# Reordering loads, casts and transposes in the first two batches of an attention + MoE kernel

## The chip, the cores and the metric

The kernel runs on one core of a Trainium2 chip. The metric is the device time of one execution in microseconds (us). Each kernel was executed four times or more, the kernel before beside it on the same chip; medians are quoted, and the spread of one kernel is mostly about 1%.

Names used below: PE is the TensorE, PEld its weight loads, DVE the VectorE, ACT the ScalarE, POOL the GpSimd, SP the engine that issues most DMAs. "The software queue" is the DMA queue that POOL issues to (q0 in the profile), "the hardware queue" the one that SP issues to (q1). Both feed the same 16 DMA engines: from 20 to 40 us of the kernel before, the profile gives them shares of 89.8% and 33.9% of these 16 (a share adds up the time that packets took, so two can exceed 100% together).

## The reference

```python
# q, k, v: (8 batches, 8 heads, 576 tokens, 64), float32
scores = q @ k.T / sqrt(64) - slope[head] * |i - j|
attn   = softmax(scores where 0 <= i - j < 128)          # a sliding window of 128
x      = (attn @ v) as 4608 tokens x 512
h      = x @ w_in                                        # 512 x 2048
out    = (h * clip(h + 3, 0, 6) / 6) @ w_out             # 2048 x 512
```

## The kernel before

The 8 batches are worked off as 32 pairs of heads, 4 for each batch (pair 4 is the first of batch 1, pair 8 the first of batch 2). For each pair PE computes scores, ACT the exponentials, POOL the masks (`affine_select`), PE the product with v. Matmuls of the MoE half fill the PE between these steps from pair 4 on.

q and k must be transposed. In batches 0 and 1 they come by the software queue (which casts to bf16 on the way), DVE reorders them into `pr`, and PE transposes. From batch 2 on SP loads them as float32, POOL casts them into the one buffer `tbuf`, and a DMA transpose writes `qTb` or `kTb`. Because `tbuf` is shared, k's cast has to wait for q's transpose.

```python
ldbuf = [...]                     # 4 load buffers, given out in turn
def load_runs(b, hs):             # q, k of batches 0, 1: software queue, 768-byte runs
    for nm in "qk": nc.gpsimd.dma_start(out=ld[b, nm][:, hs, :], in_=...)
def load_tokens(b, nm):           # v always, q and k from batch 2: hardware queue
    for j in range(NQ): nc.sync.dma_start(out=t[:n, j, :, :], in_=...)   # 256-byte runs
def load_weights_out():           # 4.2 MB float32 in, 2.1 MB bf16 landed, software queue
    for g in range(4):
        nc.gpsimd.dma_start(out=w_out_sb[:, ts(g, 4), :], in_=...)       # 1024-byte runs
def xbar(b, nm):                  # 0.66 MB, hardware queue
    nc.sync.dma_start_transpose(out=dst, in_=tbuf)
...
def prepare(g):
    ...                                    # DVE: pr of q and of k
    cast_v(b, hs, nc.gpsimd)               # POOL: v of this pair
...
def stage_next(g):                         # at the end of pair g
    b, hp = divmod(g, NP)
    if g == 0:
        new_runs(1); load_runs(1, slice(0, H)); load_tokens(1, "v")
    if g == 1:
        load_weights_out()
    if b == 1:
        if hp == 1: load_tokens(2, "v")
        if hp in (1, 2): xbar(2, "qk"[hp - 1])
        if hp < 3: cast_tokens(2, "qkv"[hp])
    if b >= 2 and b + 1 < B:
        if hp < 2: xbar(b + 1, "qk"[hp])
        if hp in (0, 2): cast_tokens(b + 1, "kkv"[hp])
    if b >= 1 and b + 2 < B:
        if hp > 0: load_tokens(b + 2, "qkv"[hp - 1])
        if hp == 3: cast_tokens(b + 2, "q")
...
new_runs(0); load_tokens(0, "v"); constants()
for hp in range(NP): load_runs(0, slice(2 * hp, 2 * hp + 2))
load_weights_in()                          # 2.1 MB landed, software queue
first_batch()
load_tokens(2, "q"); load_tokens(2, "k")
...
```

In these traces each engine works through its own instructions in program order, and what waits holds up what stands behind it on that engine: below, a cast of v on POOL that waits 2.66 us for its load has the first mask behind it. SP's issues queue in the same way.

The softmax here doesn't subtract the row's maximum and nothing guards it: scores larger than these inputs give would overflow.

## Time and profile before

| | kernel before |
|---|---|
| time, median of the first 3 runs | 373.6 us |
| scores of pair 2 / 4 / 8 start | 24.5 / 46.2 / 83.1 us |
| first mask | 18.97 us |
| k of batch 1 landed | 36.6 us |

The page's overview of the kernel before: the span in 40 slices of 9.3 us, each digit the busy share of a slice in tenths; DMA is the mean busy share of the 16 DMA engines, GB/s what they moved.

```profile
PE   1456765666998699979999999999999999999995
...
DMA  9999997999399959995998999531131010010012
GB/s 158 195 198 192 196 215 117 187 221 198 85 202 202 212 94 222 206 222 127 237 208 181 203 211 226 116 99 46 48 62 49 29 58 28 28 58 28 28 58 84
```

Counted from 0, PE is at 9 from slice 18 on (168 us) until the tail: this part is bound by PE, and what is saved earlier should come off the total. In slices 0 to 9 (to 93 us) PE is at 1 to 7, and DMA stands at 9 in all of them but the last.

The same by stages (length, then busy us and number of instructions of PE, PEld, DVE, ACT, POOL, then the granted clock, the DMA share and GB/s):

```profile
core 0: us, PE busy (x) PEld busy (x) DVE busy (x) ACT busy (x) POOL busy (x), PEclk, DMA share, GB/s
20.00:46.00 26.00, 17.00 (x162) 10.89 (x163) 13.83 (x31) 7.67 (x15) 16.37 (x30) 1.00 1.24 196
46.00:84.00 38.00, 24.13 (x241) 13.64 (x244) 21.17 (x37) 20.02 (x38) 22.18 (x41) 0.82 1.01 185
84.00:130.00 46.00, 37.16 (x315) 18.28 (x320) 20.07 (x42) 26.08 (x49) 23.94 (x43) 1.00 1.03 181
```

The clock column needs care at the start. It reads 1.00 from 20 to 46 us, yet the eight score matmuls of pair 2 took 0.61 us together, against 0.40 at pair 5. So the recorded 1.00 of the first batch does not fit the pace of its matmuls.

In 20 to 84 us PE works 41 of 64 us. By the sums of its waits there, 5.7 us are for `g` of DVE (3.3 of these behind `pr` copies that took 3.50 us beside POOL's casts) and 4.8 us for POOL's masks. The change goes at two chains. The first, on POOL in the first batch (start, length, instruction, count, in brackets the idle time before it and what ended it):

```profile
17.93 0.29 POOL L143 CAST vbuf<-ldbuf 64x128 bf16<-64x128 f32 x1 [2.66 <-DMA ldbuf<-in_v_dram]
...
18.97 1.22 POOL L218 TENSOR_SCALAR_AFFINE_SELECT pd<-pd 128x512 bf16<-128x512 bf16 x2
...
27.54 3.00 POOL L136 DMA_DIRECT2D w_out_sb<-in_moe_w_out_dram  x4
```

The masks of pair 0 (line L218) stand behind the casts of v, and these behind v's landing; ScalarE's first exponentials ran from 11.02 us. The issues of w_out then take 3.0 us ahead of pair 2's masks.

The second, on SP (start, time until the next issue, instruction) and on PE, in batch 1:

```profile
56.85 10.57 SPq L106 DMA_DIRECT2D ldbuf<-in_v_dram  x5
67.52 3.88 SPq L161 DMA_TRANSPOSE qTb<-tbuf  x1
```

```profile
76.53 0.24 PE L251 MATMUL av<-vbuf,pd 128*128 128x65 bf16 x1 [2.49 <-POOL pd L218]
```

The transpose of q (67.52) stands behind the load of v on SP. POOL's cast of k waits for that transpose, pair 6's masks stand behind that cast, and PE waits for the mask at 76.53.

These are the two DMA queues from 20 to 40 us (packets, MB landed, share of the engines), and the loads of v issued or landing in that stretch, with their time from issue to landing:

```profile
q0 software_dynamic: 3360, 2.96, 89.8%
q1 hardware_dynamic: 3667, 0.92, 33.9%
...
ldbuf<-in_v_dram SPq DMA_DIRECT2D x2, 256.0 KB, 22.2
```

The software queue (w_in, q, k, w_out) and the hardware queue (v, and q of batch 2 from 32.5 us on) moved about as many packets, 3360 and 3667, but 2.96 against 0.92 MB. (k of batch 1 took 13.5 us from its issue at 23.14 us.)

### The profile page before, as it was taken

To read this page: it belongs to the slowest core of one execution; us is meant where nothing else is said; L and a number is where in the kernel's file an instruction comes from. 1 tells how busy PE (TensorE), PEld (TensorE's weight loads), DVE (VectorE), ACT (ScalarE), POOL (GpSimd) and SP (SyncE) were. 2 spreads that over 40 slices of the span, in tenths; PEclk is the share of its full clock that TensorE was granted. 3 is DMA by queue.
4 is the path that set the end of the run, shared out by engine and by line. 5 is a ranking of instruction groups with operands and counts; after the bars stand their busy time and mean duration, and the time that the engine had idled before them with its cause. 6 is when DMAs were issued, how large, how long until landed. Compare 5 with 4: busy or idle time off the path is not lost.

```text
span 373.4 us, 6509 instructions
## 1 busy us (share of the span) xinstructions
PE 315.8 (85%) x2408; PEld 160.3 (43%) x2445; DVE 174.2 (47%) x355; ACT 198.5 (53%) x361; POOL 155.3 (42%) x279
## 2 busy tenths in 40 slices
PE   1456765666998699979999999999999999999995
PEld 0334433333444345544544554455445444444442
DVE  5355456634643244545545544555445534434410
ACT  1733264545773366757776666767666343443401
POOL 7398155195555255626674762663332000000000
PEclk9999996969999989999999999999999999999999
DMA  9999997999399959995998999531131010010012
GB/s 158 195 198 192 196 215 117 187 221 198 85 202 202 212 94 222 206 222 127 237 208 181 203 211 226 116 99 46 48 62 49 29 58 28 28 58 28 28 58 84
DMA packets 153135, 51.64 MB, mean 138 GB/s; under 512 B 141200, under 2 KB 148624, under 8 KB 153104
## 3 DMA queue, kind: packets, MB, share of 16 engines
q1 hardware_dynamic: 145504, 44.54, 61.9%
q0 software_dynamic: 7456, 6.55, 10.8%
q8 instruction: 19, 0.31, 0.4%
q10 hardware_dynamic: 144, 0.13, 0.1%
q14 instruction: 12, 0.10, 0.1%
HBM read 36.70 MB, written 9.44 MB: 124 GB/s over the span
## 4 chain that ended last, share of the span: by engine, by line
PE 62%; DVE 8%; ACT 8%; issue 7%; POOL 7%; DMA 6%; SPq 1%; another core or an unknown queue 0%; POOLq 0%
PE ops L303 28%; PE hps L286 28%; ACT r L290 4%; DVE g L291 3%; DMA ldbuf<-in_v_dram 3%; DMA xT<-avs 3%; POOL pd L218 2%; ACT po L225 2%; PE av L251 2%; PE av L248 2%; PE scd L195 2%; POOL po L230 2%; DVE avs L257 1%; DVE osb L317 1%; PE sco L202 1%
## 5 line engine op out<-in xcount | busy, mean ns | idle before, releaser
L291 DVE SCALAR_TENSOR_TENSOR g<-r,hps 128x512 bf16<-128x512 f32 x144 | 99.1, 688 | 146.5 <-ACT r L290 146.4
L290 ACT ACTIVATE r<-hps,bias 128x512 f32<-128x512 f32 x144 | 99.5, 691 | 118.8 <-PE hps L286 115.4
L286 PE MATMUL hps<-xT,w_in_sb 128*128 128x512 bf16 x552 | 151.5, 390 | 11.0 <-DMA xT<-avs 5.2
L303 PE MATMUL ops<-w_out_sb,g 128*128 128x512 bf16 x563 | 144.0, 380 | 5.6 <-DVE osb L317 3.9
L303 PEld LDWEIGHTS <-g 128*128 128x128 bf16 x576 | 55.7, 98 | 78.0 <-issue 13.9
L286 PEld LDWEIGHTS <-w_in_sb 128*128 128x128 bf16 x576 | 52.5, 100 | 59.9 <-issue 11.4
L218 POOL TENSOR_SCALAR_AFFINE_SELECT pd<-pd 128x512 bf16<-128x512 bf16 x64 | 39.3, 636 | 50.3 <-ACT pd L215 50.3
L156 POOL CAST tbuf<-ldbuf 128x512 bf16<-128x512 f32 (+1 forms) x60 | 34.0, 610 | 43.1 <-issue 36.2
L230 POOL TENSOR_SCALAR_AFFINE_SELECT po<-po 128x512 bf16<-128x512 bf16 x64 | 40.0, 633 | 20.5 <-ACT po L225 17.7
L215 ACT ACTIVATE pd<-scd,bias_d 128x512 bf16<-128x512 f32 x64 | 40.7, 684 | 12.2 <-POOL pd L218 11.2
L225 ACT ACTIVATE po<-sco,bias_o 128x512 bf16<-128x512 f32 x64 | 44.1, 690 | 0.0
L248 PE MATMUL av<-vbuf,po 128*128 128x65 bf16 x256 | 27.1, 203 | 8.2 <-DVE avs L257 6.2
L251 PE MATMUL av<-vbuf,pd 128*128 128x65 bf16 x256 | 27.0, 205 | 7.2 <-POOL pd L218 7.2
L257 DVE TENSOR_TENSOR avs<-av,rc 128x384 bf16<-128x384 f32 x64 | 31.4, 491 | 2.2
L251 PEld LDWEIGHTS <-pd 128*128 128x128 bf16 x256 | 21.2, 104 | 17.6 <-POOL pd L218 8.2
L248 PEld LDWEIGHTS <-po 128*128 128x128 bf16 x256 | 20.8, 104 | 14.4 <-DVE avs L257 9.2
L256 DVE RECIPROCAL rc<-av 128x6 f32<-128x6 f32 x64 | 11.8, 184 | 23.6 <-PE av L251 23.4
L183 PE MATMUL tp<-ident,pr 96*128 96x96 bf16 x96 | 8.8, 255 | 16.1 <-DVE pr L171 10.4
L315 ACT COPY osb<-ops 128x512 f32<-128x512 f32 x18 | 10.5, 585 | 19.3 <-PE ops L303 19.3
L228 ACT ACTIVATE p4buf<-sco,bias_d 128x64 bf16<-128x64 f32 x64 | 20.7, 324 | 0.0
L317 DVE COPY osb<-ops 128x512 f32<-128x512 f32 x17 | 11.6, 684 | 7.4 <-PE ops L303 7.4
L195 PE MATMUL scd<-qTb,kTb 64*128 64x128 bf16 x256 | 13.6, 229 | 1.8 <-DVE kTb L185 1.0
(45 smaller groups left out, 150.1 us busy)
## 6 DMA issues: line engine op xcount, KB each, us to landing
out_dram<-osb SPq DMA_DIRECT2D x35, 256.0 KB, 2.3
ldbuf<-in_v_dram SPq DMA_DIRECT2D x32, 256.0 KB, 4.9
ldbuf<-in_q_dram SPq DMA_DIRECT2D x24, 256.0 KB, 4.7
ldbuf<-in_k_dram SPq DMA_DIRECT2D x24, 256.0 KB, 5.0
w_in_sb<-in_moe_w_in_dram POOLq DMA_DIRECT2D x4, 512.0 KB, 14.0
w_out_sb<-in_moe_w_out_dram POOLq DMA_DIRECT2D x4, 512.0 KB, 16.3
ldbuf<-in_v_dram SPq DMA_DIRECT2D x8, 128.0 KB, 4.7
ldbuf<-in_q_dram SPq DMA_DIRECT2D x6, 128.0 KB, 4.7
```

Of the source, the lines that this page charges most:

```text
L156: nc.gpsimd.tensor_copy(out=tbuf[:m, :, j, :], in_=s[:m, j, :, :].rearrange("p (i e) d -> p i (e d)", e=2))
L215: nc.scalar.activation(out=pd[:, e, :, :].rearrange("p j c -> p (j c)"), in_=sc[:, e, :], func=ACT.Exp, bias=bias_d[:, h:h + 1], scale=scale)
L218: nc.gpsimd.affine_select(out=pd[:, e, :, :], in_=pd[:, e, :, :], pattern=[[0, 4], [1, 128]], channel_multiplier=-1, base=0, compare_op=AL ...
L225: nc.scalar.activation(out=po[:, e, :, :].rearrange("p j c -> p (j c)"), in_=sc[:, e, :], func=ACT.Exp, bias=bias_o[:, h:h + 1], scale=scale)
L230: nc.gpsimd.affine_select(out=po[:, e, :, :], in_=po[:, e, :, :], pattern=[[0, 4], [-1, 128]], channel_multiplier=1, base=-1, compare_op=A ...
L248: nc.tensor.matmul(av[:, i, e, :], lhsT=po[:, e, qt - 1, :], rhs=vb[:, qt - 1, h, :], start=True, stop=False)
L251: nc.tensor.matmul(av[:, i, e, :], lhsT=d, rhs=vb[:, qt, h, :], start=(qt == 0), stop=True)
L257: nc.vector.tensor_tensor(out=st[g, "avs"][:, qts[0]:qts[0] + nq, :, :], in0=av[:, 0:nq, :, 0:D], in1=rc[:, 0:nq, :, :].to_broadcast([128, ...
L286: nc.tensor.matmul(hps, lhsT=w_in_sb[:, ks, ts(ms, 128)], rhs=xT[:, ks, ts(nt, NT)], start=(ks == 0), stop=(ks == n_ks - 1))
L290: nc.scalar.activation(out=r6, in_=hps, func=ACT.Relu, bias=bias3[:, 0:1], scale=1.0 / 6.0)
L291: nc.vector.scalar_tensor_tensor(out=gts[nt][:, ms, :], in0=r6, scalar=1.0, in1=hps, op0=ALU.min, op1=ALU.mult)
L303: nc.tensor.matmul(ops[nt, sub], lhsT=gts[nt][:, ms, ts(sub, 128)], rhs=w_out_sb[:, ms, :], start=(ms == 0), stop=(ms == n_ms - 1))
```

## The change

The intent: let pair 0's masks go first by moving v's casts and w_in's issues behind them; keep w_out out of the crowded first 50 us; and in batch 1 let q and k of batch 2 go through the transposes before v of batch 2 and w_out are loaded. Buffers are given out by name (`slot_of`), so that the order of loads is free; the buffers are the same.

```diff
+    def slot_of(b, nm): ...
 def prepare(g):
     ...
-        cast_v(b, hs, nc.gpsimd)
 def stage_next(g):
+        if b == 0:
+            cast_v(0, slice(2 * hp, 2 * hp + 2), nc.gpsimd)
         if g == 0:
-            new_runs(1)
+            load_weights_in()
+        if g == 1:
             load_runs(1, slice(0, H))
-            load_tokens(1, "v")
-        if g == 1:
-            load_weights_out()
         if b == 1:
+            if hp == 0:
+                cast_tokens(1, "v")
             if hp == 1:
+                cast_tokens(2, "q")
+                xbar(2, "q")
+            if hp == 2:
+                cast_tokens(2, "k")
+                xbar(2, "k")
                 load_tokens(2, "v")
-            if hp in (1, 2):
-                xbar(2, "qk"[hp - 1])
-            if hp < 3:
-                cast_tokens(2, "qkv"[hp])
+                load_weights_out()
+            if hp == 3:
+                cast_tokens(2, "v")
 ...
         load_tokens(0, "v")
+        new_runs(1)
+        load_tokens(1, "v")
 ...
-        load_weights_in()
         first_batch()
```

More of the change, by code (lines that the diff above doesn't have):

```diff
@@ L81, with slot_of @@
     kTb = [held.tile([128, NP, NQ, 128], BF16, name=f"kTb{i}") for i in range(2)]
-    ld, nld = {}, [0]
+    ld = {}
     src_of = {"q": q, "k": k, "v": v}
-    def next_ld():
-        nld[0] += 1
-        return ldbuf[(nld[0] - 1) % 4]
+    def slot_of(b, nm):
+        if b < 2:
+            return 2 * b + (1 if nm == "v" else 0)
+        return (3 * (b - 2) + "qkv".index(nm)) % 4
     def new_runs(b):
-        t = next_ld()[:, :].bitcast(BF16)
+        t = ldbuf[slot_of(b, "q")][:, :].bitcast(BF16)
         for n, nm in enumerate("qk"):
@@ L101, in load_tokens @@
     def load_tokens(b, nm):
-        t = next_ld()[:, 0:NQ * H * D].rearrange("p (j h d) -> p j h d", j=NQ, h=H)
+        t = ldbuf[slot_of(b, nm)][:, 0:NQ * H * D].rearrange("p (j h d) -> p j h d", j=NQ, h=H)
         ld[b, nm] = t
```

## The prediction

> **What bounds the kernel now.** The table of stages has two regimes. From 140 us on the TensorE is busy 96 to 99% of nearly every stage until the tail: time saved earlier passes straight through. From 0 to 130 us it is busy only 84 us; the change touches only this part.
>
> Before, as the timelines show it:
> 1. First batch. ScalarE has finished the exponentials of pairs 0 and 1 by 17.9 us, but GpSimd, which runs in order, sits on the casts of v (landed at 14.6 and 17.9 us), so the first mask starts at 18.97 us. ScalarE idles 7.3 us, TensorE 4 us. Then 3.0 us of issuing w_out delays pair 2's masks (30.5 us). The batch ends at 39.8 us.
> 2. The 16 DMA engines are saturated from 4 to 60 us (about 195 GB/s): w_in and w_out share the first 50 us with q, k and v. The second batch's k lands 13.5 us after issue, at 36.7 us.
> 3. Second batch (scores at 46.2, 51.8, 63.8, 71.7, the third's first at 83.1 us). GpSimd's casts collide with VectorE's pr copies: two take 3.50 us together, otherwise 0.35 each; TensorE waits 3.3 us. The Trainium skill, "GPSIMD Engine Reference", Key points, says that the two share SBUF interfaces; this trace agrees. The transpose of batch 2's q stands behind the load of v on the sync queue (issued at 67.5 us), k's cast waits 7.7 us for it, and pair 6's masks behind that stall TensorE 2.5 us at 74 us. Its granted clock falls to 0.78 to 0.88 in 50 to 90 us.
>
> **What the change does.** No arithmetic is added.
> - Masks of pair 0 start near 11.8 us, 7 us earlier. w_in's issues (3 us on GpSimd) now stand between pairs 0 and 1. With 2.8 us of masks and 0.9 of casts for each pair, 3 for w_in and 1.6 for q and k, GpSimd ends near 31 us instead of 35.8: the batch could end 5 us earlier.
> - But w_in is issued 8 us later, ahead of batch 1's q and k, and batch 2's q load starts early and competes. From the bytes and 160 GB/s for that queue I estimate k of batch 1 at 35 to 38 us, so only 1.5 to 4 us of the 5 survive.
> - Second batch: the pair-6 stall (about 3.5 us, and cold clock) goes; the collision at 54 us shrinks by 1 us, but another appears one pair later (about 1.3 us). New critical link: cast q (2.8), transpose (5.2), cast k (2.8), transpose (5.2) must finish before the third batch's scores, which I expect 5 us earlier than before, near 78 us.
> - New cost: batch 2's v is loaded only after k's transpose, beside w_out (2.1 MB landing, some 13 us of all engines). Its cast stands ahead of pair 8's masks on GpSimd; I estimate 0 to 6 us of TensorE stall there.
>
> Net: -5 plus 1 to 4 of new stall, less perhaps a microsecond of warmer clock: 369 us, range 361 to 376. Faster by over 2% 0.30, within 2% 0.64, slower 0.06.
>
> **What would show it.** First mask near 12 us; scores of pair 2 near 19 instead of 24.5 us; first w_in matmuls near 38 to 41 instead of 41.7; no wait at pair 6's masks; scores of pair 8 near 78; GpSimd waiting for v before pair 8's masks, and TensorE for that mask. After that the same pace as before, shifted.
>
> **What would make it wrong.** k of batch 1 landing much earlier (near 362) or later; v of batch 2 landing without delay (near 364); the transposes slowed by w_out, so that pair 8's scores stall (375 or more).

## The result

The kernel after took 387.6 us (385.8 to 390.2, four runs), the kernel before 373.2 us: slower by 4.0%, ratio 1.040 (95% interval 1.032 to 1.048). Ratios in this document are the mean time of one kernel's fast runs over that of the other's of the same rounds, so they are not quite the ratio of the medians quoted.

| us | before | after |
|---|---|---|
| first mask | 18.97 | 11.46 |
| scores of pair 2 | 24.5 | 18.4 |
| k of batch 1 landed | 36.6 | 41.0 |
| scores of pair 4 | 46.2 | 47.3 |
| scores of pair 7 | 71.7 | 71.2 |
| scores of pair 8 | 83.1 | 92.7 |
| scores of pair 11 | 110.3 | 123.6 |
| scores of pair 31 | 280.6 | 295.7 |

The overview of the kernel after (slices of 9.7 us now):

```profile
PE   1753757703889779997999999999999999999986
...
DMA  9999900999979996999799799951212101001012
GB/s 167 205 197 192 188 1 3 196 191 208 200 130 225 193 220 95 220 206 181 148 232 212 156 225 201 186 129 46 66 51 46 45 29 54 27 29 54 27 56 81
```

DMA is at 0 in slices 5 and 6 (49 to 68 us), where it was at 9 before, and PE is at 0 in slice 8. The stages of the kernel after, and below them two stretches around the hole:

```profile
20.00:46.00 26.00, 12.90 (x116) 7.94 (x114) 9.48 (x23) 6.45 (x14) 10.40 (x21) 1.00 1.20 198
46.00:84.00 38.00, 22.27 (x229) 12.10 (x226) 20.43 (x38) 20.29 (x39) 22.46 (x37) 0.93 0.54 91
84.00:130.00 46.00, 31.93 (x249) 15.33 (x250) 16.98 (x35) 22.71 (x42) 21.08 (x35) 0.84 1.11 194
```

```profile
80.00:90.00 10.00, 0.00 (x0) 0.00 (x0) 0.00 (x0) 0.00 (x0) 0.82 (x2) 0.59 1.22 196
90.00:100.00 10.00, 4.83 (x48) 2.81 (x49) 2.42 (x6) 3.41 (x7) 2.07 (x3) 0.67 1.25 203
```

From 80 to 90 us PE, DVE and ACT do nothing, and the clock sinks. The Trainium skill, "TensorE: Matmul & The Clock Gate", Part 1, says that an idle window of about 3.4 us halves the clock. This trace agrees: PE ran dry at 77.7 us, and the granted clock was 1.00 until 81 us and 0.50 from 82 us until after PE worked again (95 us).

The first batch went as intended. POOL in the kernel after:

```profile
11.46 1.23 POOL L218 TENSOR_SCALAR_AFFINE_SELECT pd<-pd 128x512 bf16<-128x512 bf16 x2 [4.70 <-ACT pd L215]
...
15.45 3.00 POOL L131 DMA_DIRECT2D w_in_sb<-in_moe_w_in_dram  x4
...
22.79 0.78 POOL L98 DMA_DIRECT2D ldbuf<-in_k_dram  x1
```

Masks first, then the cast of v (already there), then w_in's issues. But k of batch 1 is issued at 22.79 us behind all of w_in, and DVE waits for q and k at the start of batch 1, where the kernel before had them lying ready (first fence: before, second: after):

```profile
39.76 0.61 DVE L171 COPY pr<-ldbuf 96x768 bf16<-96x768 bf16 x2
```

```profile
36.54 0.36 DVE L172 COPY pr<-ldbuf 96x768 bf16<-96x768 bf16 x1 [2.48 <-DMA ldbuf<-in_q_dram]
40.98 0.36 DVE L172 COPY pr<-ldbuf 96x768 bf16<-96x768 bf16 x1 [4.08 <-DMA ldbuf<-in_k_dram]
```

So the first batch ended 5.8 us earlier (last copy to `xT` at 33.6 us instead of 39.4), and the start of batch 1 was 1.1 us later. Batch 1 then ran well up to pair 7. SP and PE in the kernel after:

```profile
70.46 4.44 SPq L107 DMA_DIRECT2D ldbuf<-in_q_dram  x5
75.24 6.99 SPq L162 DMA_TRANSPOSE kTb<-tbuf  x1
```

```profile
92.71 0.61 PE L195 MATMUL scd<-qTb,kTb 64*128 64x128 bf16 x8 [15.00 <-DMA kTb<-tbuf]
```

PE waited 15.00 us for the transpose of k. It was issued at 75.24 us and took 17.4 us to land. In the kernel before, the same transpose, issued at 75.95 us with no software-queue traffic beside it:

```profile
kTb<-tbuf SPq DMA_TRANSPOSE x1, 5.4
```

While the transpose of the kernel after was under way, the queues from 78 to 90 us:

```profile
q0 software_dynamic: 1843, 1.84, 90.8%
q1 hardware_dynamic: 1848, 0.47, 31.2%
...
kTb<-tbuf SPq DMA_TRANSPOSE x1, 17.4
```

The packets are equal to within 5, the bytes are 3.9 to 1. w_out had been issued by POOL at 75.16 us, in the same breath as the transpose.

### The profile page after: what moved, and what is told of

It reads as the page before. It is cut to its first block, busy times and chain, and to the rows that moved or that the text cites. A ratio compares the mean times of both kernels' runs of the same rounds, so it can differ in the third digit from the quotient of the medians.

```text
span 388.5 us, 6543 instructions
## 1 busy us (share of the span) xinstructions
PE 320.5 (83%) x2445; PEld 161.1 (41%) x2445; DVE 172.0 (44%) x355; ACT 198.6 (51%) x361; POOL 155.3 (40%) x274
## 4 chain that ended last, share of the span: by engine, by line
PE 58%; DMA 13%; SPq 7%; POOL 7%; issue 6%; ACT 4%; DVE 4%; POOLq 0%
PE ops L303 27%; PE hps L286 25%; SPq L107 7%; DMA ldbuf<-in_k_dram 5%; DMA ldbuf<-in_v_dram 3%; DMA xT<-avs 3%; DMA qTb<-tbuf 3%; ACT r L290 2%; POOL tbuf L157 2%; POOL pd L218 2%; PE av L251 2%; PE scd L195 1%; PE av L248 1%; DVE g L291 1%; POOL po L230 1%
## 5 line engine op out<-in xcount | busy, mean ns | idle before, releaser
L286 PE MATMUL hps<-xT,w_in_sb 128*128 128x512 bf16 x576 | 155.0, 394 | 8.4 <-DMA xT<-avs 5.6
L303 PE MATMUL ops<-w_out_sb,g 128*128 128x512 bf16 x576 | 146.4, 382 | 4.7 <-DVE osb L317 3.9
L303 PEld LDWEIGHTS <-g 128*128 128x128 bf16 x576 | 55.9, 98 | 79.1 <-issue 15.5
L215 ACT ACTIVATE pd<-scd,bias_d 128x512 bf16<-128x512 f32 x64 | 40.8, 685 | 6.5 <-POOL po L230 3.9
L251 PE MATMUL av<-vbuf,pd 128*128 128x65 bf16 x256 | 26.1, 204 | 2.7 <-POOL vbuf L143 2.0
L251 PEld LDWEIGHTS <-pd 128*128 128x128 bf16 x256 | 21.4, 105 | 13.3 <-issue 4.0
L150 POOL CAST vbuf<-ldbuf 128x1024 bf16<-128x1024 f32 x14 | 14.4, 1053 | 17.1 <-DMA ldbuf<-in_v_dram 17.1
L195 PEld LDWEIGHTS <-kTb 64*128 64x128 bf16 x256 | 7.9, 100 | 29.0 <-DMA kTb<-tbuf 15.2
```

Source lines behind the costliest of these rows:

```text
L215: nc.scalar.activation(out=pd[:, e, :, :].rearrange("p j c -> p (j c)"), in_=sc[:, e, :], func=ACT.Exp, bias=bias_d[:, h:h + 1], scale=scale)
L251: nc.tensor.matmul(av[:, i, e, :], lhsT=d, rhs=vb[:, qt, h, :], start=(qt == 0), stop=True)
L286: nc.tensor.matmul(hps, lhsT=w_in_sb[:, ks, ts(ms, 128)], rhs=xT[:, ks, ts(nt, NT)], start=(ks == 0), stop=(ks == n_ks - 1))
L303: nc.tensor.matmul(ops[nt, sub], lhsT=gts[nt][:, ms, ts(sub, 128)], rhs=w_out_sb[:, ms, :], start=(ms == 0), stop=(ms == n_ms - 1))
```

## The experiments

The theories after the result. **W**: w_out's transfer beside the transpose took the DMA engines from it. **Q**: the transpose stood on the hardware queue behind the load of batch 3's q, issued 5 us earlier. For the first half, **O**: k of batch 1 is late because all of w_in stands ahead of it on the software queue; **C**: it is late because the load of batch 2's q competes on the other queue. Twelve kernels ran, three timed rounds each, all with correct results; the first four on one chip (before 374.97 us), the next four on another (372.93), the last four again together (373.58). Medians are of all runs of a kernel.

| run | median us | ratio to before [95%] | scores of pair 4 / 8 at |
|---|---|---|---|
| e1_wout_early | 374.85 | 1.002 [0.996, 1.008] | 46.7 / 79.9 |
| e2_q3_behind | 398.02 | 1.066 [1.058, 1.073] | 46.7 / 90.3 |
| e3_neither | 385.74 | 1.033 [1.026, 1.041] | 47.1 / 79.8 |
| e4_first_half | 376.77 | 1.007 [1.002, 1.013] | 47.6 / 84.8 |
| e5_ring_order | 372.18 | 0.996 [0.992, 1.001] | 40.8 / 74.0 |
| e6_k_first | 377.32 | 1.007 [0.999, 1.016] | 44.8 / 77.8 |
| e7_v_early | 379.31 | 1.017 [1.012, 1.021] | 47.7 / 81.1 |
| e8_all | 367.21 | 0.983 [0.978, 0.988] | 40.3 / 73.6 |
| e9_wout_first_pair | 381.58 | 1.021 [1.015, 1.028] | 47.6 / 84.1 |
| e10_half_wout | 383.65 | 1.027 [1.022, 1.033] | 46.9 / 86.2 |
| e11_small_packets | 396.93 | 1.063 [1.057, 1.069] | 46.9 / 86.7 |
| e12_v3_behind | 367.45 | 0.985 [0.981, 0.989] | 41.5 / 74.6 |

(The profile of e6 is of a slow run, 379.3 us; its table entries of places and its readings below are used only for the first 45 us. One of e9's four runs was slow too. The medians of the fast runs alone are 376.3 us for e6 and 380.1 us for e9.)

### Which neighbour held the transpose: e1, e2, e3

e1, on the kernel after:

```diff
         if g == 1:
             load_runs(1, slice(0, H))
+            load_weights_out()
 ...
                 load_tokens(2, "v")
-                load_weights_out()
```

> The kernel after with w_out issued in the first batch again (behind q and k of batch 1), all else as after. In after the transpose of batch 2's k took 17.4 us from issue to landing and the TensorE stood 15.0 us for it. Theory W (w_out's 2.1 MB beside the transpose took the DMA engines' time): the transpose lands in 5 to 7 us, the wait at the scores of pair 8 is under 2 us, those scores start at 77 to 80 us, time 370 to 375. Rival Q (the transpose stood in the sync queue behind the load of batch 3's q, 1.2 MB issued 5 us earlier): the wait is hardly shorter, 8 us or more, time above 380.

e2, on the kernel after (w_out stays):

```diff
                 load_weights_out()
+                load_tokens(3, "q")
 ...
-            if hp > 0:
+            if hp > (1 if b == 1 else 0):
                 load_tokens(b + 2, "qkv"[hp - 1])
```

> The kernel after with the load of batch 3's q moved behind k's transpose and v's load; w_out still beside the transpose. Theory W: the transpose is still slow (10 us or more), a wait of 6 us or more stays at the scores of pair 8, time 379 to 386. Rival Q: the transpose lands in 5 to 7 us, the wait is under 2 us, time 371 to 376. If both are needed together, a wait of 2 to 5 us stays.

e3 has both edits, with the load of batch 3's q directly behind that of batch 2's v.

> Both of it: w_out early and batch 3's q behind the transpose. Both theories: transpose in 5 us, no wait at pair 8, scores of pair 8 at 77 to 79 us, time 369 to 373. What this kernel is still slower or faster than before is what the rest of the change is worth.

Measured: without w_out beside it, but with the load of q still ahead, k's transpose landed in 5.3 us, and PE waited 2.9 us for it instead of 15.0 (e1; I had expected less than 2, so the transpose still ends last at pair 8). With w_out beside it and nothing ahead it took 17.0 us and PE waited 14.5 us (e2). The queues of e1 from 78 to 90 us, and of e2 from 78 to 88 us:

```profile
q1 hardware_dynamic: 9586, 2.41, 99.7%
...
kTb<-tbuf SPq DMA_TRANSPOSE x1, 5.3
```

```profile
q0 software_dynamic: 1558, 1.55, 91.1%
q1 hardware_dynamic: 1555, 0.40, 29.8%
...
kTb<-tbuf SPq DMA_TRANSPOSE x1, 17.0
```

The hardware queue alone moved 2.41 MB in 12 us, 201 GB/s; beside w_out 0.40 MB in 10 us, 40 GB/s. W stands, Q falls: without the load ahead the transpose was no faster to speak of (17.0 against 17.4 us). The arithmetic closes too: 0.66 MB at 39 GB/s (the 0.47 MB in 12 us of the kernel after) is 17 us.

The times of e2 and e3 were missed, e3's badly (385.7 against 369 to 373), and the reason is my own edit. In both kernels the load of batch 3's q comes after v's, while its cast stands ahead of pair 8's masks on POOL and its transpose ahead of k's cast. In e3, POOL waited 11.3 us for that transpose before k's cast of batch 3, and the scores of pair 10 started 15.5 us after those of pair 9, where before it was 9.7. So these two kernels settle the transpose, but not the time; the 2x2 design was confounded.

e1 shows what the rest of the change is worth: nothing that can be measured, 1.002. It is 3.2 us ahead of before at pair 8 and 0.7 us behind at pair 31.

### Is it packets? e10 and e11

If the two queues take turns packet by packet, the transpose's rate follows from packet sizes, not from bytes waiting.

```diff
# e10: half of w_out stays beside the transpose, half goes early
+            load_weights_out([0, 1])      # at g == 1
-                load_weights_out()
+                load_weights_out([2, 3])
# e11: same bytes, time and place; 256-byte runs in place of 1024
-                out=w_out_sb[:, ts(g, 4), :],
-                in_=moe_w_out[ds(g * 512, 512), :].rearrange("(m p) d -> p m d", p=128))
+                out=w_out_sb[:, :, ts(g, 128)],
+                in_=moe_w_out[:, ts(g, 128)].rearrange("(m p) d -> p m d", p=128))
```

> The kernel after with half of w_out issued in the first batch and half (1.05 MB) left beside k's transpose. In after the two queues moved 1843 and 1848 packets between 78 and 90 us, 1.84 and 0.47 MB: packet for packet, 1 KB against 256 bytes. Theory P (turns by packet): the transpose, 0.66 MB of 256-byte packets, moves at about 40 GB/s while w_out runs, some 7 us, and at about 200 GB/s after that: it lands in 8.5 to 11 us instead of 17.4, the wait at pair 8 is 6 to 9 us, time 377 to 382. Rival S (the transpose simply stands still until w_out has landed, or any load beside it costs it the same): it lands in 12 us or more, or in 17 again.

> The kernel after with w_out's four loads cut by columns instead of rows, so that each packet lands 256 bytes instead of 1 KB; bytes, place and time of issue as in after. Theory P: the queues still take turns packet for packet, but with equal bytes, so k's transpose moves at 80 to 100 GB/s: it lands in 7 to 9.5 us instead of 17.4, the wait at pair 8 falls from 15 to 4 to 8 us, time 376 to 383. Rival B (each queue gets its share by bytes or w_out goes first): 15 us or more as before, time 385 to 391. w_out itself may land later than in after.

Measured, e10: the transpose landed in 11.4 us, between the ranges of P (8.5 to 11) and S (12 or more); PE waited 9.0 us, and the time, 383.7 us, was above P's range. The landing alone does not decide. The queues do: from 78 to 81 us, with w_out in full flow, they moved 467 packets each, and the hardware queue 0.12 MB, which is the 40 GB/s of P. The transpose did not stand still. The queues of e11 from 76 to 88 us:

```profile
q0 software_dynamic: 3681, 0.94, 78.0%
q1 hardware_dynamic: 3961, 1.00, 62.8%
...
kTb<-tbuf SPq DMA_TRANSPOSE x1, 11.6
```

Now the packets are again nearly equal, and so are the bytes, 0.94 and 1.00 MB; from 80 to 86 us, with both queues busy throughout, they are equal, 2013 and 2013. With w_out's bytes, issue and place unchanged, the transpose landed in 11.6 us instead of 17.4. That shows equal turns by packet, and refutes a share by bytes or w_out going first. It missed the range of 7 to 9.5 us, because both queues together moved only 162 GB/s (after: 190 in the same stretch). PE still waited 9.5 us (expected 4 to 8), and the time got worse (396.9 us), not better, because w_out's last piece now took 25 us to land and held up the loads of v and k behind it. Small packets are no remedy; they only show the mechanism.

The Trainium skill, "DMA: Bandwidth & Descriptors", Queues, rings and completion order, says that each DMA engine serves the queues in turn, packet by packet. This trace agrees in that the counts are equal: 1843 against 1848 packets. But the page's packet is a group of some 9 to 17 descriptors (a descriptor is one piece of a transfer), while a packet of the profile is, by its bytes, one run of 1 KB or 256 bytes. How many runs an engine takes from one queue before it turns to the other, no run here shows.

### Another place for w_out: e9

The DMA engines of the kernel after stand idle from 49 to 68 us, so one line can move:

```diff
             if hp == 0:
                 cast_tokens(1, "v")
+                load_weights_out()
 ...
-                load_weights_out()            # in hp == 2
```

> The kernel after with one line moved: w_out issued in batch 1's first pair, behind v's cast, where the DMA engines of after are idle (1 to 3 GB/s around 48 to 68 us), instead of in the third pair. Theory W: w_out has all engines for most of its 2.1 MB (about 10.5 us at 200 GB/s), the transpose of k lands in 5 to 7 us, the wait of 15 us at pair 8 falls below 5 us; the transpose of q, issued at 67 us, meets the tail of w_out and is 1 to 4 us late. Time 374 to 379. If the place of w_out is not what costs, it stays at 384 or more.

Measured: 380.1 us over the fast runs, some 7 us better than the kernel after but above the range. k's transpose landed in 5.1 us, yet q's, issued at 67.3 us, met the tail of w_out and took 8.7 us; k's cast waited 4.0 us for it, and PE still waited 6.3 us at pair 8 (expected: below 5). POOL, busy with v's casts, had issued w_out only from 58.13 us on, so that too little of the idle stretch (49 to 68 us) was left for it.

### The first half: e4, e5, e6

e4 has only the first batch of the change; batch 1 as in the kernel before, w_out issued behind q and k of batch 1.

> Only the first half of the change: masks ahead of v's casts and w_in behind pair 0's masks in batch 0; batch 1 as in the kernel before, w_out issued behind batch 1's q and k. My reading of after: w_in issued 8 us later, and batch 2's q load beside it, hold back k of batch 1 to 40 to 41 us, so that the scores of pair 4 start at 46 to 48 us as before and nothing is gained: time 372 to 376. The prediction's view: k of batch 1 lands at 35 to 38 us, the scores of pair 4 start 1.5 to 4 us earlier, time 368 to 371.

Measured: 376.8 us (a little above my range), scores of pair 4 at 47.6. The earlier masks alone are worth nothing; the kernel is even 0.7% slower. e5 and e6 then ask what holds k back, on e1:

```diff
# e5 (w_out moves two pairs later too)
         if g == 0:
-            load_weights_in()
+            load_weights_in([0])          # one quarter
+            load_runs(1, slice(0, H))
         if g == 1:
-            load_runs(1, slice(0, H))
-            load_weights_out()
+            load_weights_in([1, 2, 3])
+        if g == 3:
+            load_weights_out()
# e6
-        load_tokens(2, "q")
         load_tokens(2, "k")               # its buffer is free only at 30 us
+        load_tokens(2, "q")
```

> e1_wout_early, where the first batch's masks ran earlier but k of batch 1 landed only at 41 us, with GpSimd's loads in another order: one quarter of w_in, q and k of batch 1, then the other three quarters and w_out. Theory O (k stands behind all of w_in in GpSimd's queue): k lands before the first batch ends near 34 to 37 us, TensorE no longer waits for the pr copies of pair 4, scores of pair 4 start at 40 to 43 us instead of 46.7, time 368 to 372 against 374.9 of e1. If the place in that queue is not what holds it, the scores stay at 46 to 47 us and the time at 374 to 376.

> e1_wout_early with the loads of batch 2's q and k swapped on the sync queue: k's buffer comes free only at 30 us, so that no load of the sync queue runs beside w_in and batch 1's q and k from about 18 to 30 us. Theory C (competition of that load holds back k of batch 1): k lands at 33 to 36 us instead of 41, scores of pair 4 at 42 to 44 us; the time gains less than that, as batch 2's q then lands later: 370 to 375. Theory O alone: k still lands at 39 us or later, scores of pair 4 at 46 to 47 us.

Measured, e5: k landed at 30.5 us, earlier than expected, and pair 4's pr copies did not wait any more (this is DVE at the start of batch 1):

```profile
33.70 0.61 DVE L172 COPY pr<-ldbuf 96x768 bf16<-96x768 bf16 x2
```

Scores of pair 4 at 40.8 us, 5.9 earlier than in e1, and 5.9 earlier at pair 8, 5.6 at pair 31: it comes through whole in the profiled run (370.2 us). The median of its four runs is 372.2; the other three had a clock of 0.968 instead of 0.981. The ratio to before is 0.996, which is not clear of 1. e5 also issues w_out two pairs later than e1; in e1 it stood behind k on the same queue, but I did not test the two moves apart.

Measured, e6: with the hardware queue nearly silent (0.15 MB from 20 to 34 us), the software queue moved 2.66 MB in these 14 us. That is 190 GB/s, against 156 in e1 in the same stretch (2.19 MB). k landed at 37.4 us and the scores of pair 4 started at 44.8 instead of 46.7, both between what C and what O alone had forecast. So C is true as well, but worth 2 us where O is worth 6. e6's time did not gain (1.007, not clear of 1; I had expected 370 to 375 us).

### What else batch 1's order costs: e7, e8, e12

In e1 POOL waited 5.5 and 2.7 us for batch 2's v ahead of pair 8's masks, and 6.8 us for the transpose of batch 3's q ahead of pair 9's. e7 loads v between the transposes of q and k, with batch 3's q behind k's. e8 combines e5, e7, and batch 3's v behind batch 3's first transpose:

```diff
# e7, on e1
                 xbar(2, "q")
+                load_tokens(2, "v")
 ...
                 xbar(2, "k")
-                load_tokens(2, "v")
+                load_tokens(3, "q")           # and not at its old place, as in e2
# e12, on e5; e8 has this, e5 and e7
             if hp < 2:
                 xbar(b + 1, "qk"[hp])
+            if g == 2 * NP:
+                load_tokens(3, "v")
 ...
-            if hp > 0:
+            if hp > 0 and (b, hp) != (1, 3):
                 load_tokens(b + 2, "qkv"[hp - 1])
```

> e1_wout_early with the load of batch 2's v put between the transposes of q and k, and batch 3's q behind k's transpose. In e1 GpSimd waited 5.5 and 2.7 us for v before pair 8's masks. My theory: that wait goes, pair 8's masks end near 86 instead of 93 us, but the cast of batch 3's q now waits for its load by 2 to 5 us; scores of pair 8 near 77 to 80 us, time 371 to 375. In e3, where both loads stood behind k's transpose, it was 385.7; if v's place makes no difference, this is 380 or more.

> A version to beat both: e5's order of GpSimd's loads, e7's place of v, and batch 3's v behind the transpose of batch 3's q instead of ahead of it. Scores of pair 4 at 40 to 42 us, of pair 8 at 71 to 75 us, time 362 to 368. If the gains of e5 and e7 do not add, because GpSimd's casts behind batch 3's loads then set the pace, 369 to 374.

> e5_ring_order with only batch 3's v moved behind the transpose of batch 3's q on the sync queue; batch 2's v stays where e5 has it. In e5 that transpose was issued at 89.2 us, 4 us after its cast, behind two loads, and GpSimd waited 6.6 us for it ahead of pair 9's masks. My theory: this part is what makes e8 5 us faster than e5: scores of pair 11 about 28 us behind those of pair 8 instead of 31.8, time 367 to 370. If it is v's early place that counts, no gain over e5: 371 to 373.

Measured, e7: 379.3 us, outside the range, 1.017 against e1's 1.002; scores of pair 8 at 81.1 (expected 77 to 80). v's cast no longer waited, but the cast of batch 3's q then trickled in with its load until 89.1 us, and k's cast waited 9.6 us for the transpose behind it. The wait was moved, not removed.

e8: 367.2 us, 0.983: it beats both kernels. e12 shows where its gain over e5 comes from. POOL's cast of batch 3's k, in e5 (first) and e12:

```profile
94.62 2.84 POOL L157 CAST tbuf<-ldbuf 128x512 bf16<-128x512 f32 x5 [6.59 <-DMA qTb<-tbuf]
```

```profile
91.63 2.83 POOL L157 CAST tbuf<-ldbuf 128x512 bf16<-128x512 f32 x5 [2.52 <-DMA qTb<-tbuf]
```

The wait for q's transpose sank from 6.59 to 2.52 us, because that transpose no longer stands behind the load of v on SP. Scores of pair 11 came 29.6 us behind those of pair 8 (e5: 31.8; I had expected about 28), and the time was 367.5 us, 0.985, as good as e8 within the noise (measured in different rounds). v's early place, which e8 has and e12 has not, adds nothing that these runs can show.

## Why the prediction was wrong

It gave 369 us (361 to 376) and 6% to a result slower by over 2%; measured 387.6, slower by 4%.

- *First mask near 12 us, scores of pair 2 near 19, batch 0 ending 5 us earlier*: right (11.46, 18.4, 5.8 us).
- *k of batch 1 at 35 to 38 us, 1.5 to 4 us of the 5 survive*: mechanism right, size wrong. k landed at 41.0 us. The term was the rate of the software queue, taken as 160 GB/s; it moved only 0.32 MB from 15 to 20 us (the hardware queue, with v of batch 1, 0.67) and 148 GB/s from 20 to 40 us. The 3.3 MB of w_in, q and k that stand up to k's end are then through at 40 us. All of the gain was lost, and 1.1 us more (e4, e5, e6).
- *The pair-6 stall goes, the collision with DVE's copies shrinks*: right. Pair 6's masks started at 67.15 us instead of 75.84, and PE did not wait for them; what that is worth shows in e1, where from pair 7's scores to pair 8's took 9.4 us, before 11.4. The two copies in the collision took 1.84 us instead of 3.50, and from pair 5's scores to pair 7's took 18.2 us, before 19.9. The predicted new collision one pair later is there but small: two copies took 1.17 us instead of 0.61, and it cost nothing that shows (pair 6 to 7: 7.85 us, before 7.86).
- *"Transpose (5.2) ... must finish before the third batch's scores, which I expect ... near 78 us"*: this is the step that failed. The chain was named rightly as the new critical link, but costed with durations from a stretch without w_out. k's transpose took 17.4 us beside w_out, scores of pair 8 started at 92.7. The 12.0 us above before's 5.4 account for nearly all of the 12.8 us to e1's start of pair 8 (79.9, close to the prediction), and e1, e2 and e10 show the cause.
- *A stall of 0 to 6 us for v ahead of pair 8's masks*: POOL did wait, 14.6 us, but PE hardly noticed, since it was waiting for the transpose itself.
- *"The transposes slowed by w_out" was listed under what would make it wrong*, with 375 or more. The suspicion was there, the arithmetic was not: the kernel before shows the hardware queue at 0.92 MB in 20 us, 46 GB/s, and a load of v at 22.2 us beside the software queue. 0.66 MB at 46 GB/s is 14 us.

The rest of the loss is smaller. After minus before is 9.6 us at pair 8 and 11.3 at pair 9 (cold clock: four matmuls of 512 columns took 1.89 us there against 1.02 warm). It is 13.3 at pair 11: pair 9's masks started 11.7 us after pair 9's scores, before 6.8. They stood behind k's cast, which waited 6.4 us for batch 3's transpose of q, issued at 106.9 us behind three loads on SP. That wait is not new (before: 6.9 us). What is new is that it began later, because q's cast stood behind v's, and v's had waited 14.6 and 2.5 us for the load beside w_out. e12 shows on e5 that the transpose's place on SP matters; the late cast of q I did not test. The last 2 us appear at pair 18, after a wait of 2.30 us (before: 1.84) for `xT`, with a lower clock behind it (0.66 from 180 to 185 us); I did not test this.

What stays open: the 2 us at pair 18, the share of q's late cast in the 2 us before pair 11, and whether e6's order gains anything in time.

## What to carry to other kernels

Cost a DMA with its duration beside the traffic that it will have, not with its median over the run: two busy queues shared the engines by packets, so that a queue of 256-byte packets fell to a fifth of its rate beside one of 1024-byte packets. Place a bulk load by who waits for the other queue at that time, and order each queue by deadline: here one line's move of w_out (e1 against after, 1.002 against 1.040) was worth more than 3%, and one quarter of w_in ahead of q and k, the rest behind, brought pair 4's scores 5.9 us forward (e5 against e1; in time this was clear of 1 only together with e12's order on SP). An engine that finishes earlier only helps if what it then waits for is earlier too.

## What the Trainium skill lacked or had wrong

- "DMA: Bandwidth & Descriptors", Queues, rings and completion order: it has the turns by packet, but not what follows for bytes. Measured: 1843 packets of 1 KB against 1848 of 256 bytes in 12 us, 1.84 against 0.47 MB; the hardware queue fell from 201 (e1) to 39 GB/s (a fifth), not to a half. The page's packet is a group of descriptors; the packets whose counts are equal here are single runs.
- The same page, Rules for kernel authors, says of correctness that "A transpose next to ordinary DMAs needs nothing". In time it can need a lot: 17.4 us instead of 5.3 beside 2.1 MB of w_out.
- The same page, Issuing engine by pattern, calls the hardware path "generally faster". Its section on the two paths speaks of faster setup; neither says which path gets the bytes when both are busy. In this kernel the software queue took 2.96 of 3.88 MB from 20 to 40 us before and 1.84 of 2.31 MB from 78 to 90 us after, where both were busy throughout, by its larger packets; with packets of 256 bytes on both (e11) the shares were 0.94 and 1.00 MB.
